# A routed expert kernel: the first token search without its filler products, its grids on ScalarE, and a second expert whose later weight loads wait for its rows

## The chip, the cores and the metric

The kernel runs on one core of a Trainium2 chip. It is one program, launched once. The metric is the device time of one execution in microseconds. Engines are named as in the profile: PE is TensorE, DVE is VectorE, ACT is ScalarE, POOL is GpSimd and SP is SyncE, which here only issues transfers.

## What is computed

An attention stage, then a routing that gives every token one of eight experts, then the experts, then a second feed-forward stage with shared weights, in float32:

```python
x = attention(q, k, v, M_prev, z_prev, beta)      # 4 x 576 tokens, 8 heads of 64
logits = x @ w_gate                               # 2304 tokens, 8 experts
for idx in argsort(-logits.flatten()):            # best pair of token and expert first
    tok, e = divmod(idx, 8)
    if token not assigned and counts[e] < 288:
        assigned[tok] = e; counts[e] += 1
for e in range(8):
    out[mask_e] = maximum(x[mask_e] @ w1[e], 0) @ w2[e]
h = maximum(maximum(out @ m2w1, out @ m2w2), out @ m2w3)
y = h @ m2wo
```

## The kernel before

The program has two parts. `attention` computes the tokens' rows `x` (sent to HBM as `xd`) and their logits `L`. The second part, `routing` and `experts`, runs eight rounds: in each, a search on DVE and PE finds which expert fills up next and which 288 tokens it gets; three indirect transfers on POOL (the gathers, L1223) fetch those tokens' rows; PE transposes them (L1270); then come the two products of the expert (`h1` into `w`, `y` into `acc`) and the second stage (`m2` into `w`, `o` into `acc`). Every product is three matmuls (L1282 to L1284), since each operand is split into a high and a low part: ACT rounds the high part and DVE subtracts it.

**What sets the order.** The parts are written as tasks with a key, costs on their engines and the tasks they depend on (`plan.add`, `plan.op`). `Plan.run` simulates the engines with these costs and writes out one fixed order per engine, and each engine's queue is in order. A changed cost, key or latency therefore changes the order that is written. `GLAT` is the latency that the planner assumes behind a gather, `WLAT` behind a weight load, and `R1KEY` the key at which the second round's search stands.

**The search.** A round has several steps. One step compares all tokens' best logits with a grid of thresholds (`cq`, L1003, in the first round three pieces of 6 token blocks), counts on PE how many lie above each for each expert (L1011, six matmuls per piece), compares the counts with the room left (`fl`, L1015), sums the flags on PE (L1021), takes the maximum (`n1`, L1030) and shifts the logits (`res`, L1032). The next step needs the shifted logits, so the steps are one chain. The first round has six steps of 32 thresholds; its grids `kst` and negated steps `ns` are written by POOL (L964 and L980), apart from the first grid, which DVE writes. A last pass numbers the chosen tokens (L1074, L1082) and gives the row numbers `tidx` (L1088) for the gathers. Before the first step the largest logit `am` goes through PE twice (L941, L955) to reach all partitions.

**The filler.** `NFILL` products of a tile of ones with itself (L1178) are planned wherever PE would be free during the first round's search, and 18 more (`PRE`) stand ahead of it. Nobody reads their result.

**Raw weight pieces.** During attention the second stage's weights, which lie in HBM as 64-bit numbers, are read in 24 pieces into `m2raw` (one buffer) and turned into float32 by one ACT (L818) and three DVE operations (L822, L825, L828). An expert's own weights come in eight pieces of 512 KB (`wraw`, three buffers, L1241) issued by SP. For the first expert only, pieces 3 and later wait for the gathered rows (`FL0`, `tg0`).

Of the kernel before, what the change touches and what calls it, by code (L numbers as in the profile page):

```python
# [17 lines left out]
try:  # L18
# [4 lines left out]
F32 = mybir.dt.float32  # L23
# [22 lines left out]
FL0 = 3  # L46
NFILL, PRE = 398, 18
R1, R1KEY = 9, 15
# [3 lines left out]
GLAT, WLAT = 2500, 6000  # L52
# [4 lines left out]
        "nmt": 2, "PT": 2, "st": 5, "r5": 2, "tmp": 1, "rm": 2, "x": 2, "g": 2, "m2raw": 1, "m2a": 1, "m2b": 1}  # L57
# [3 lines left out]
        "T": (-1.2, 4.7, 5.8), "qj": "POOL", "nslack": 600, "A": (4.1, 6.4, 7.6, 8.7, 8.8), "norm": 15.3, "gate": 6, "m2": (0.0, 5.9, 13.5),  # L61
# [781 lines left out]
def routing_consts(g, tc, consts):  # L843
# [7 lines left out]
    g.iota = iota("iota_row", [128], [[1, 128]], 1)  # L851
    g.w8 = iota("w8", [E], [[-1, E]], E)
# [31 lines left out]
def routing(g, tc, plan, rt, rps, L):  # L884
# [74 lines left out]
    def Q(c, f, r, w):  # L959
        return plan.op(at(), {"POOL": c}, lambda e: f(), r.split(), w.split())  # L960

    def grid(i, s, on=Q, v=nc.gpsimd):
        n, b = PLANS[i]
        on(180 + 1.2 * 2 ** b, lambda: v.tensor_scalar(  # L964
            kst[i][:, s], g.iota[:, :2 ** b], -2.0 ** (b - 1) if s == 0 else -1.0 if s == n - 1 else 0.0, st[i][:, s:s + 1],
            op0=OP.add, op1=OP.mult), f"st{i}", f"kst{i}{s}")

    for i in range(2):
        V(65, lambda i=i: v.tensor_scalar(st[i], g.pw[i], am, None, op0=OP.mult), "am", f"st{i}")
        if i == 0:  # L970
            grid(0, 0, V, v)
# [4 lines left out]
    for i, (n, b) in enumerate(PLANS):  # L976
        for s in range(n):
            if i or s:
                grid(i, s)
            Q(180, lambda i=i, s=s: nc.gpsimd.tensor_scalar(ns[i][:, s], st[i][:, s:s + 1].to_broadcast([128, NB]), -1.0, None,  # L980
                                                            op0=OP.mult), f"st{i}", f"ns{i}{s}")
# [6 lines left out]
    for ph in range(E):  # L988
# [7 lines left out]
        if ph < E - 1:  # L996
# [4 lines left out]
            for s in range(n):  # L1001
                for a in range(0, NB, q):
# [10 lines left out]
                    P(30 * w + (60 if ph else 0), cnt, " ".join(f"cq{x}" for x in range(a + q - w, a + q, q)) + " ohU" +  # L1013
# [59 lines left out]
        for a in range(0, NB, q):  # L1073
# [10 lines left out]
            r.ti = P(46 * w + (60 if ph else 0), idx, " ".join(f"cq{x}" for x in range(a + q - w, a + q, q)) + " mov0 mov1 mov2" +  # L1084
# [26 lines left out]
def experts(g, tc, plan, top, wr, xd, idxd, out):  # L1111
# [60 lines left out]
    def warm(n):  # L1172
        def f(e):
            if not hasattr(fo_, "t"):
                ps.tile([128, 512], F32, name="w", bufs=FBUFS["w"])
                fo_.t = ps.tile([128, 512], F32, name="acc", bufs=4)
            for _ in range(n):
                nc.tensor.matmul(fo_.t[:, :128], g.ones, g.ones, start=True, stop=True)  # L1178
        return f
# [359 lines left out]
```

## Time and profile before

| What | Value |
|---|---|
| median of 3 runs | 874.17 us (873.16 to 878.25) |
| the profiled execution, device time | 874.84 us |
| the profiled execution, span of the core | 872.1 us |
| PE busy | 834.8 us, 96% of the span |
| DVE busy | 553.7 us, 63% |
| ACT busy | 338.9 us, 39% |
| POOL busy | 108.1 us, 12% |
| mean granted PE clock | 0.986 of full speed |

The 2.7 us between the profiled time and its span lie outside the core's instructions. The span has four stretches: attention up to about 266 us, the first search and the gathers of the first expert up to about 309 us, then the experts up to about 866 us, then the last stores. A line of the timeline gives start, duration, engine, line of the kernel, operation, output and inputs, the count of merged instructions, and in brackets how long the engine had idled and for whom. PE's matmuls overlap in it, so a group's duration is the issue of all of them and the drain of the last.

### The profile page before, as it was taken

How to read it: one execution, taken by the hardware profiler on the slowest of the kernel's cores; microseconds unless marked ns; L12 is line 12 of the kernel's file. 1: busy time of each engine (PE TensorE's matmuls, PEld its weight loads, DVE VectorE, ACT ScalarE, POOL GpSimd, SP SyncE). 2: the span in 40 equal slices, each digit the busy share in tenths (PEclk: the TensorE clock that was granted, in tenths of full speed). 3: DMA queues.
4: the chain of work that ended last, by engine and by line, in shares of the span. 5: the costliest groups of instructions: out<-in, count | busy, mean ns of one | idle time of the engine just before them, and what ended most of it. 6: DMA issues, size and time to landing. Idle time of an engine off the chain costs nothing.

```text
span 872.1 us, 18532 instructions
## 1 busy us (share of the span) xinstructions
PE 834.8 (96%) x7234; PEld 770.8 (88%) x7234; DVE 553.7 (63%) x1607; ACT 338.9 (39%) x843; POOL 108.1 (12%) x257
## 2 busy tenths in 40 slices
PE   8899999999997999979999999999999999999996
PEld 6788888888887898869999999999999999999996
DVE  7577777878756796947884783773675552532321
ACT  2566656656555332213313313412412422422311
POOL 2221121123113200202002002002002001000001
PEclk9999999999998999979999999999999999999998
DMA  5445554554323560504403403401421441430000
GB/s 152 142 132 175 167 155 134 187 168 137 122 72 104 140 152 6 170 28 135 111 1 125 121 2 100 126 22 64 145 50 52 145 50 52 145 49 26 25 1 36
DMA packets 39288, 85.59 MB, mean 98 GB/s; under 512 B 11552, under 2 KB 13728, under 8 KB 39200
## 3 DMA queue, kind: packets, MB, share of 16 engines
q1 hardware_dynamic: 35648, 72.87, 29.4%
q0 software_dynamic: 3552, 11.54, 4.6%
q8 instruction: 56, 0.92, 0.4%
q14 instruction: 32, 0.26, 0.1%
HBM read 72.77 MB, written 9.45 MB: 94 GB/s over the span
## 4 chain that ended last, share of the span: by engine, by line
PE 70%; issue 16%; DVE 7%; ACT 4%; POOL 1%; DMA 1%; DVEq 0%; POOLq 0%; ACTq 0%
PE av L622 12%; PE w L1282 9%; PE w L1284 9%; PE w L1283 9%; PE st L582 5%; PE acc L1282 4%; PE acc L1283 4%; PE acc L1284 4%; PE mem L529 3%; PE mem L481 2%; ACT x L552 2%; PE acc L1178 2%; PE rps L1011 2%; DMA xg<-xd,tidx 1%; ACT pt L608 1%
## 5 line engine op out<-in xcount | busy, mean ns | idle before, releaser
L1282 PE MATMUL w<-yh,mh 128*128 128x288 f32 x576 | 174.1, 302 | 0.0
L1284 PE MATMUL w<-yh,ml 128*128 128x288 f32 x576 | 170.0, 295 | 0.0
L1283 PE MATMUL w<-yl,mh 128*128 128x288 f32 x576 | 169.7, 295 | 0.0
L622 PE MATMUL av<-V,pt 128*128 128x112 f32 (+1 forms) x960 | 112.1, 265 | 0.3 <-DVE r L689 0.3
L1282 PEld LDWEIGHTS w<-yh,mh 128*128 128x128 f32 x576 | 109.0, 189 | 2.6
L1283 PEld LDWEIGHTS w<-yl,mh 128*128 128x128 f32 x576 | 108.6, 189 | 2.8
L622 PEld LDWEIGHTS av<-V,pt 128*128 128x128 f32 (+1 forms) x960 | 98.2, 173 | 13.4 <-issue 8.5
L1284 PEld LDWEIGHTS w<-yh,ml 128*128 128x128 f32 x576 | 108.5, 188 | 0.0
L1252 DVE TENSOR_TENSOR wlo<-wraw,whi 128x1024 fp32r<-128x1024 f32 x64 | 78.2, 1222 | 32.3 <-ACT whi L1248 32.3
L1389 DVE TENSOR_TENSOR mt<-w,mt 128x288 f32<-128x288 f32 x96 | 43.6, 455 | 79.2 <-PE w L1284 77.3
L422 DVE CUSTOM_DVE_ANT_0 junk<-st,mask 128x512 bf16<-128x512 f32 (+2 forms) x144 | 66.2, 460 | 30.3 <-PE st L409 20.7
L1283 PE MATMUL acc<-hl,whi 128*128 128x288 f32 x256 | 76.1, 297 | 1.3 <-DVE hl L1197 0.9
L1248 ACT CAST whi<-wraw 128x1024 fp32r<-128x1024 f32 x64 | 67.1, 1049 | 24.5 <-PE acc L1283 16.2
L1284 PE MATMUL w<-xhi,wlo 128*128 128x288 f32 x256 | 75.7, 296 | 0.9 <-DVE wlo L1252 0.9
L1282 PE MATMUL acc<-hh,whi 128*128 128x288 f32 x256 | 76.2, 298 | 0.0
L1282 PE MATMUL w<-xhi,whi 128*128 128x288 f32 x256 | 75.9, 296 | 0.1
L1283 PE MATMUL w<-xlo,whi 128*128 128x288 f32 x256 | 75.5, 295 | 0.0
L1284 PE MATMUL acc<-hh,wlo 128*128 128x288 f32 x256 | 75.3, 294 | 0.0
L1130 ACT CAST gc<-mt 128x32 fp32r<-128x32 f32 (+2 forms) x72 | 17.5, 243 | 141.5 <-DVE mt L1389 141.5
L1223 POOL DMA_INDIRECT xg<-xd,tidx x24 | 25.0, 1042 | 353.4 <-PE w L1284 181.1
L1197 DVE SCALAR_TENSOR_TENSOR hl<-w,hh 128x288 fp32r<-128x288 f32 x64 | 29.1, 456 | 60.2 <-ACT hh L1191 60.2
L608 ACT ACTIVATE pt<-st 128x512 f32<-128x512 f32 x96 | 52.3, 605 | 24.5 <-PE st L582 23.6
(233 smaller groups left out, 1771.4 us busy)
## 6 DMA issues: line engine op xcount, KB each, us to landing
wraw<-in_wr SPq DMA_DIRECT2D x64, 512.0 KB
m2raw<-in_m2w SPq DMA_DIRECT2D x12, 512.0 KB
V<-in_v SPq DMA_DIRECT2D x16, 365.0 KB
KR<-in_kN SPq DMA_DIRECT2D x16, 288.0 KB
QN<-in_qN SPq DMA_DIRECT2D x16, 288.0 KB
VT<-in_vT SPq DMA_DIRECT2D x16, 288.0 KB
xd<-x SPq DMA_DIRECT2D x16, 256.0 KB
m2raw<-in_m2w SPq DMA_DIRECT2D x12, 256.0 KB
```

The costliest lines, as they stand in the source:

```text
L422: V.tensor_tensor_reduce(out=junk[:, :w], in0=o.s[x][:, c:c + w], in1=m, scale=1.0, scalar=-3.0e38, op0=OP.add, op1=OP.max, accum_out=r.nm ...
L529: PE.matmul(MEM[:m, 2 * C * jj:2 * C * jj + 2 * C], r.phi[:, 128 * j:128 * j + m], r.MZ, start=True, stop=True)
L582: PE.matmul(d[:kr, c:c + z - a], neg[q, :kr] if wt is None else wt[q, k], mv[q, a:z], start=x == 0, stop=x == 3)
L608: A.activation(r.PT[:, i, 512 * gi:512 * gi + 512], o.t[i], AF.Exp, scale=0.125)
L622: PE.matmul(AV[:m, i, j * C:j * C + w], r.PT[:, i, o:o + m], r.V[:, c:c + w], start=kb == 0, stop=kb == j)
L1197: V.scalar_tensor_tensor(lo(), src(), 0.0, hi().bitcast(F32), op0=OP.max, op1=OP.subtract)
L1248: A.copy(x.W[fb][0], x.RAW[fb])
L1252: V.tensor_sub(x.W[fb][1], x.RAW[fb], x.W[fb][0].bitcast(F32))
L1282: nc.tensor.matmul(o, wh, rh, start=start, stop=False)
L1283: nc.tensor.matmul(o, wh, rl, start=False, stop=False)
L1284: nc.tensor.matmul(o, wl, rh, start=False, stop=stop)
L1389: V.tensor_max(q.mt, o.pt[:, :T], q.mt)
```

## The change

Six things change. The 18 products ahead of the search and those inside it go: 88 products of ones are left, and each may start only behind the last numbering matmul of the first round. The planner's costs of the first round's matmuls are raised. All 20 operations that write grids and negated steps go to ACT; as ACT's scaling takes no offset, three shifted rows of integers are made once by POOL during attention. `m2raw` gets a second buffer and its conversions other keys. Pieces 3 and later of the second expert wait for that expert's gathers too. `GLAT` is 8500 for all experts but the first, and `R1KEY` 12.

```diff
-NFILL, PRE = 398, 18
-R1, R1KEY = 9, 15
+NFILL = 88
+R1, R1KEY = 9, 12
...
-GLAT, WLAT = 2500, 6000
+GLAT, WLAT = 8500, 6000
...
-        "nmt": 2, "PT": 2, "st": 5, "r5": 2, "tmp": 1, "rm": 2, "x": 2, "g": 2, "m2raw": 1, "m2a": 1, "m2b": 1}
+        "nmt": 2, "PT": 2, "st": 5, "r5": 2, "tmp": 1, "rm": 2, "x": 2, "g": 2, "m2raw": 2, "m2a": 1, "m2b": 1}
...
-"m2": (0.0, 5.9, 13.5),
+"m2": (4, 6.0, 10),
...
+    g.shift = [iota(f"iota{i}", [n], [[1, n]], 1 - a, dt=BF) for i, (n, a) in enumerate([(2 ** b, 2 ** (b - 1)) for _, b in PLANS] + [(128, 1)])]
...
     def Q(c, f, r, w):
-        return plan.op(at(), {"POOL": c}, lambda e: f(), r.split(), w.split())
-
-    def grid(i, s, on=Q, v=nc.gpsimd):
+        return plan.op(at(), {"ACT": c}, lambda e: f(), r.split(), w.split())
+
+    def grid(i, s):
         n, b = PLANS[i]
-        on(180 + 1.2 * 2 ** b, lambda: v.tensor_scalar(
-            kst[i][:, s], g.iota[:, :2 ** b], -2.0 ** (b - 1) if s == 0 else -1.0 if s == n - 1 else 0.0, st[i][:, s:s + 1],
-            op0=OP.add, op1=OP.mult), f"st{i}", f"kst{i}{s}")
+        x = g.iota if 0 < s < n - 1 else g.shift[i if s == 0 else 2]
+        Q(170 + 0.89 * 2 ** b, lambda: nc.scalar.mul(kst[i][:, s], x[:, :2 ** b], st[i][:, s:s + 1]), f"st{i}", f"kst{i}{s}")
...
         if i == 0:
-            grid(0, 0, V, v)
+            grid(0, 0)
...
-            Q(180, lambda i=i, s=s: nc.gpsimd.tensor_scalar(ns[i][:, s], st[i][:, s:s + 1].to_broadcast([128, NB]), -1.0, None,
-                                                            op0=OP.mult), f"st{i}", f"ns{i}{s}")
+            Q(190, lambda i=i, s=s: nc.scalar.mul(ns[i][:, s], st[i][:, s:s + 1].to_broadcast([128, NB]), -1.0), f"st{i}", f"ns{i}{s}")
...
-                    P(30 * w + (60 if ph else 0), cnt, " ".join(f"cq{x}" for x in range(a + q - w, a + q, q)) + " ohU" +
+                    P((30 if ph else 50) * w + (60 if ph else 0), cnt, " ".join(f"cq{x}" for x in range(a + q - w, a + q, q)) + " ohU" +
...
-            r.ti = P(46 * w + (60 if ph else 0), idx, " ".join(f"cq{x}" for x in range(a + q - w, a + q, q)) + " mov0 mov1 mov2" +
+            r.ti = P((46 if ph else 95) * w + (60 if ph else 0), idx, " ".join(f"cq{x}" for x in range(a + q - w, a + q, q)) + " mov0 mov1 mov2" +
...
-    tf = add(-2000, {"PE": 1}, warm(PRE), new=[bfl])
     for k in range(NFILL):
-        add(1e5 + k, {"PE": 56}, warm(1), [tf], use=[bfl])
+        add(1e5 + k, {"PE": 75}, warm, [g.rounds[0].ti], new=[] if k else [bfl], use=[bfl] if k else [])
...
-                          [r.tt], new=[bg] if c == 0 else [], use=[bg] if c else [], lat=GLAT))
-        if p == 0:
-            tg0 = tg
+                          [r.tt], new=[bg] if c == 0 else [], use=[bg] if c else [], lat=GLAT if p else 2500))
...
-                if p == 0 and fb == FL0:
+                if p < 2 and fb == FL0:
...
-            t0 = add(kw + FK["load"] + .1, {"SP": 2000}, fl, [x.tvl] + (tg0 if p == 0 and fb >= FL0 else []), new=[br], lat=WLAT)
+            t0 = add(kw + FK["load"] + .1, {"SP": 2000}, fl, [x.tvl] + (tg if p < 2 and fb >= FL0 else []), new=[br], lat=WLAT)
```

The order shows what the planner made of this at three places. The first is DVE at the end of attention, from the last logits to the first operation of the search (`am`); `tmp` and `x` are the last head's rows. Before, and then now:

```order
L707 TENSOR_TENSOR L<-L,lg_3877 64x8
L723 TENSOR_TENSOR tmp<-av,r_3861 128x10x64
L727 TENSOR_TENSOR x<-x,tmp 128x2x5x64
L822 TENSOR_SCALAR m2b<-m2raw 128x512
L825 SCALAR_TENSOR_TENSOR m2b<-m2a,m2b 128x512
L828 SCALAR_TENSOR_TENSOR w_80<-m2raw,m2b 128x512
L939 TENSOR_REDUCE am<-L 128x1
```

```order
L707 TENSOR_TENSOR L<-L,lg_3889 64x8
L723 TENSOR_TENSOR tmp<-av,r_3873 128x10x64
L727 TENSOR_TENSOR x<-x,tmp 128x2x5x64
L940 TENSOR_REDUCE am<-L 128x1
```

The last conversion of a raw piece stands no longer between them; the last of the 24 conversions now stands some 60 DVE instructions ahead of `am`, and the first some 35 earlier than before.

The second is PE from the spreading of `am` to the first count (27 products of ones stand where the line of dots is), and now the same and, behind the dots, the end of the first round up to the transposes of the first expert's rows (`xg`):

```order
L955 MATMUL rps<-one_3094,am_3917 128x1
L1178 LDWEIGHTS ones
L1178 MATMUL acc<-ones 128x128
...
L1011 LDWEIGHTS cq
L1011 MATMUL rps<-ohU,cq 32x8
```

```order
L942 MATMUL rps<-ident,am 1x128
L956 MATMUL rps<-one_3132,am_3923 128x1
L1010 LDWEIGHTS cq
L1010 MATMUL rps<-ohU,cq 32x8
...
L1081 MATMUL rps<-mov,cq 96x6
L1095 LDWEIGHTS ones
L1095 MATMUL rps<-rab,ones 128x8
L1174 LDWEIGHTS ones
L1174 MATMUL acc<-ones 128x128
...
L1010 MATMUL rps<-ohU,cq 128x8
L1261 MATMUL w<-ident,xg 128x96 x12
```

No product of ones is left in the search; all 88 stand in one piece behind it, and behind them the 18 counts of the second round's first step and then the transposes, as before (where the piece of ones there had 107). On ACT the first plan's twelve grid operations stand behind two of the twelve casts of the second stage's weights, the other eight behind the last of these casts; the accumulating transfers of POOL (L1157), which were behind POOL's grids, keep their places against the gathers.

The third is PE between the second round's numbering matmuls and the transposes of the second expert's rows, before and now:

```order
L1082 MATMUL rps<-mov,cq 96x6
L1282 MATMUL w<-yh,mh_3970 128x288
...
L1284 MATMUL w<-yh,ml 128x288
L1270 MATMUL w<-ident,xg 128x96 x3
```

```order
L1081 MATMUL rps<-mov,cq 96x6
L1273 MATMUL w<-yh,mh_3977 128x288
...
L1275 MATMUL w<-yh,ml 128x288
L1261 MATMUL w<-ident,xg 128x96 x3
```

Before, 66 matmuls of 288 columns, 6 of 512 and 18 counts stand at the dots; now 90 of 288, 18 of 512 and 36 counts. From the transposes of the third expert on, PE's order is the same in both.

## Rows read from the trace of the kernel before

**Rows 1.** Windows: stretch, its length, busy us per engine, granted PE clock, DMA share, GB/s.

```profile
276.00:277.00 1.00, 1.00 (x12) 0.95 (x9) 0.00 (x0) 1.00 (x2) 1.00 (x5) 0.50 0.00 0
...
372.00:373.00 1.00, 0.00 (x0) 0.00 (x0) 0.00 (x0) 0.00 (x0) 0.00 (x0) 0.81 0.00 0
...
382.00:383.00 1.00, 1.00 (x4) 0.76 (x4) 0.98 (x2) 0.00 (x0) 0.00 (x0) 0.57 0.00 0
...
390.00:500.00 110.00, 109.93 (x921) 105.41 (x920) 79.44 (x219) 37.74 (x82) 9.84 (x13) 1.00 0.34 97
```

**Rows 2.** Timeline, from the end of attention to the search's first count.

```profile
269.13 0.42 DVE L822 TENSOR_SCALAR m2b<-m2raw 128x512 int32<-128x512 int32 x1
...
270.99 0.29 DVE L939 TENSOR_REDUCE am<-L 128x1 f32<-128x144 f32 x1
...
272.26 0.13 DVE L953 TENSOR_SCALAR am<-am 1x1 int32<-1x1 int32 x1
...
273.65 0.58 PE L955 MATMUL rps<-one,am 1*128 1x1 f32 x2
...
274.16 3.04 PE L1178 MATMUL acc<-ones 128*128 128x128 bf16 x27
...
275.00 0.91 DVE L1003 TENSOR_TENSOR cq<-m,kst 128x192 bf16<-128x192 f32 x3
...
277.92 0.31 PE L1011 MATMUL rps<-ohU,cq 128*32 128x8 bf16 x6
```

**Rows 3.** Timeline, later steps of the first round's search.

```profile
279.92 1.36 DVE L1003 TENSOR_TENSOR cq<-res,kst 128x192 bf16<-128x192 f32 x3
...
283.05 0.90 DVE L1003 TENSOR_TENSOR cq<-res,kst 128x192 bf16<-128x192 f32 x3
...
284.28 0.31 PE L1011 MATMUL rps<-ohU,cq 128*32 128x8 bf16 x6
...
284.63 0.15 DVE L1015 TENSOR_TENSOR fl<-rps,R 32x8 bf16<-32x8 f32 x1 [0.68 <-PE rps L1011]
...
285.07 0.17 PE L1021 MATMUL rps<-fl,ones 32*128 32x8 bf16 x1
...
291.61 0.90 DVE L1003 TENSOR_TENSOR cq<-res,kst 128x192 bf16<-128x192 f32 x3
...
293.93 0.17 DVE L1030 TENSOR_REDUCE n<-rps 128x1 f32<-128x8 f32 x1 [0.58 <-PE rps L1027]
```

**Rows 4.** Timeline, from the end of the first round to the first expert's transposes.

```profile
300.18 6.13 PE L1178 MATMUL acc<-ones 128*128 128x128 bf16 x107
...
300.55 0.16 DVE L1088 SCALAR_TENSOR_TENSOR tidx<-rps,ixs 96x3 int32<-96x3 f32 x1
...
306.91 1.08 PE L1270 MATMUL w<-ident,xg 96*128 96x96 f32 x9
```

**Rows 5.** Timeline, the second expert's row numbers, gathers and transposes.

```profile
357.15 0.93 PE L1082 MATMUL rps<-mov,cq 128*96 128x6 bf16 x18
...
366.55 1.27 POOL L1223 DMA_INDIRECT xg<-xd,tidx  x1 [0.31 <-issue]
...
375.12 0.42 PE L1270 MATMUL w<-ident,xg 96*128 96x96 f32 x1 [5.73 <-DMA xg<-xd,tidx]
...
376.47 0.42 PE L1270 MATMUL w<-ident,xg 96*128 96x96 f32 x1 [0.93 <-DMA xg<-xd,tidx]
```

**Rows 6.** Tile view of `xhi`, 370 to 400 us: durations min/median/max, first and last start.

```profile
L1282 PE MATMUL w<-xhi,whi x14: 292/295/378, 389.7 to 399.0; 128*128 128x288 f32 x14
```

**Rows 7.** Source view of the gathers, all 24 of them.

```profile
DMA to landing us min/median/max: 3.0/3.1/11.2
```

**Rows 8.** Waits, 20 to 266 us: us in total, times, longest.

```profile
PE st L582 <- ACT pt L608: 8.9, 14, 1.1
```

**Rows 9.** Groups on ACT: count | busy us, mean ns | idle before.

```profile
L1130 ACT CAST gc<-mt 128x32 fp32r<-128x32 f32 (+2 forms) x72 | 17.5, 243 | 141.5 <-DVE mt L1389 141.5
...
L1147 ACT CAST mh<-w 128x1024 fp32r<-128x1024 f32 x12 | 11.6, 1038 | 0.0
```

More of the change, by code (lines that the diff above doesn't have):

```diff
@@ L60 @@
 PRIO = {"load": -24, "prep": -17, "low": -9.5, "S": -18.6, "ds": 2.6, "N": -8.8, "G": -6, "phi": -4.5, "mem": (0.7, 5.0), "memx": "ACT",
-        "T": (-1.2, 4.7, 5.8), "qj": "POOL", "nslack": 600, "A": (4.1, 6.4, 7.6, 8.7, 8.8), "norm": 15.3, "gate": 6, "m2": (0.0, 5.9, 13.5),
+        "T": (-1.2, 4.7, 5.8), "qj": "POOL", "nslack": 600, "A": (4.1, 6.4, 7.6, 8.7, 8.8), "norm": 15.3, "gate": 6, "m2": (4, 6.0, 10),
         "tmg": (1, 6, 9, 12)}
@@ L1170, in experts, with warm @@
     bfl, fo_ = Buf(R["acc"]), K()
[L1172 to L1179, printed above, removed]
-    tf = add(-2000, {"PE": 1}, warm(PRE), new=[bfl])
+    def warm(e):
+        if not hasattr(fo_, "t"):
+            fo_.t = ps.tile([128, 512], F32, name="acc", bufs=4)
+        nc.tensor.matmul(fo_.t[:, :128], g.ones, g.ones, start=True, stop=True)
     for k in range(NFILL):
-        add(1e5 + k, {"PE": 56}, warm(1), [tf], use=[bfl])
+        add(1e5 + k, {"PE": 75}, warm, [g.rounds[0].ti], new=[] if k else [bfl], use=[bfl] if k else [])
     g.scat = []
@@ L1206, in experts @@
     E_ = [K() for _ in range(E)]
-    tg0 = []
     prev = None
```

## The prediction

> **What bounds the kernel now.** I read the windows first. From 390 to 500 us PE is busy 109.93 of 110 us [rows 1], and PE's order from the third expert on is untouched, so nothing there can be won or lost. Two stretches are left in which PE's work is not the bound. One is the first search, from the first operation on the logits at 270.99 us [rows 2] to the transposes of the first expert's rows at 306.91 [rows 4]: 35.9 us in which PE does little that anybody reads. The other is the second expert's start, where PE reaches the transposes and waits 5.73 and 0.93 us for two gathers [rows 5]. PE is the bound again right behind both, so what is saved in either shortens the kernel by as much. In the timeline of these stretches the reader is to look, in each step of the chain, for time between the end of one operation and the start of the next on the other engine: that is where a product of ones, a DVE conversion or a late transfer sits.
>
> **The conversions leave the tail.** `am` starts at 270.99 behind the conversion that begins at 269.13 [rows 2]; with none there it starts at 269.13: 1.86 us. The work itself moves into attention, where the 24 conversions are spread over as many DVE instructions as before, only some 35 to 60 earlier. I cost that at nothing. What covers it there is PE's own work; PE waited for exponentials on ACT 8.9 us in 14 waits [rows 8], and I allow 1.5 us either way.
>
> **The first products of ones go.** DVE has the reduced `am` ready at 272.39 (272.26 + 0.13), PE runs its matmul at 273.65 [rows 2]. With an empty queue about 0.1 us of hand-over is left: 1.15 us saved. POOL's and DVE's writing of grids becomes ACT's: an ACT operation on 32 to 96 columns takes 0.243 us on average [rows 9], DVE's first grid took about the same, and the hand-overs add at most 0.2 us; I take zero.
>
> **The steps.** A step of the search lasts (291.61 - 283.05) / 3 = 2.85 us undisturbed [rows 3]: 0.90 for the comparisons, 0.64 from their end (283.95) to the end of the third count (284.59), 0.19 to the end of the flags (284.78), 0.29 to the sum of the flags (285.07), 0.83 for the maximum, the shift and the hand-overs to the next comparison. Without ones in the queue the third count starts about 0.1 us behind its comparison and the sum 0.1 us behind the flags. At the clock of before the step would be 0.90 + 0.1 + 0.31 + 0.19 + 0.1 + 0.83 = 2.43 us.
>
> But the clock will not be that of before. In the window at 276 us it was granted at 0.50, the lower of PE's two levels (1.2 GHz), after PE had stood idle at the end of attention, and 27 products of ones then took 3.04 us, 0.112 each; at the upper level 107 took 6.13, 0.057 each [rows 1, 2, 4]. It rose only after PE had worked without a break. In the changed search PE has 18 small counts per step and waits in between, so I take the lower level for all of it. What a count costs there, no row shows. A group of six takes 0.31 us at the upper level [rows 3], of which some 0.04 us each is issue and the rest drain. Lower bound: nothing more. Upper bound: its issue doubles as that of the ones did, 0.47 per group, more than the 0.30 of a comparison; PE then paces the step, with 0.30 + 0.1 + 3 x 0.47 + 0.17 of drain to the end of the third count and 0.05 more in the sum: 3.14 us. I take 2.65, nearer to the lower end, because the issue of a count with 8 columns does not follow its columns: 0.04 against 0.057 for 128.
>
> The first step lasted 275.00 to 279.92, 4.92 us, with the count behind 27 ones (277.92), and the second 3.13, with comparisons of 1.36 instead of 0.90 us beside POOL's grids [rows 2, 3]. Gains: 4.92 - 2.65 = 2.27; 3.13 - 2.65 = 0.48; three steps of 0.20, 0.61 together; the last, from 291.61 to the maximum at 293.93, 0.22. The numbering behind it has 18 matmuls at the lower clock, of which the last six are not covered: 0.25 us lost. Row numbers: 1.86 + 1.15 + 2.27 + 0.48 + 0.61 + 0.22 - 0.25 = 6.3 us earlier, 300.55 becomes 294.2.
>
> **The 88 products behind the search.** They start where the 107 did, 300.18 - 6.3 = 293.9, and stand ahead of the counts and the transposes. After the second expert's wait the clock was still below full 6 us after PE had taken up work at 376.47 (0.57 in the window at 382 us) [rows 1, 5]. By that, 54 ones at 0.112 take 6.0 us and 34 at 0.057 another 1.9, ending at 301.8; with 0.6 for the counts the transposes start at 302.5. The rows themselves would be there at 306.91 - 6.3 = 300.6 [rows 4]: now the ones are late, not the gathers. The first product comes 306.91 - 302.5 = **4.4 us** earlier. Bounds: 9.9 us if all 88 run at 0.112, 5.0 if none does.
>
> ACT's other work is hidden: twenty grid operations are 4.9 us of ACT, which held only casts that are needed from the second stage on. They delay the third accumulating transfer, which stands ahead of the gathers in POOL's queue and behind twenty grid operations, ten casts and three negations on ACT: from the steps' values at about 271.5 that is 20 x 0.243 + 13 x 1.04 us later [rows 9], 289.9, against the new `tidx` at 294.2. Beyond these 4.3 us each us of delay is a us of the kernel.
>
> **The second expert.** Its numbering matmuls stood at 357.15, the last gather landed with the transpose at 376.47, 19.3 us later [rows 5]; the shortest landing of a gather is 3.0 us, the median 3.1, the longest 11.2 [rows 7]. Between the two PE now has 90 matmuls of 288 columns at 0.133 (the spacing in the trace), 18 of 512 at 0.229, 36 counts and the numbering itself: 18.2 us of its own work, where it had 12.0 (357.15 to 369.15). And SP's loads of pieces 3 and later, which were under way when the gather of 366.55 was issued, now wait for it. So the wait goes: 5.73 + 0.93, and with it the lower clock up to about 382.5, in which 6 us of work took the place of 3: together **9.7 us**. SP has only this expert's other pieces and its row numbers for the stores behind the waiting load. The first product is at 389.7 [rows 6], 13.2 us behind the last transposed rows; before the fourth piece is needed, 72 matmuls of the first product and at least 48 of the second run, some 16 us. Late next would be that piece, and its cover is long.
>
> **A rule against the change.** The Trainium skill (TensorE: Matmul & The Clock Gate, What's actually happening) says that the throttled state is the default and activity lifts it; by that, taking the ones out leaves the search at half rate. The rows at 276 us agree on the two rates. If everything PE does in the search doubled by it, the sum would be that of the second rival below.
>
> **The sum.** 4.4 + 9.7 = 14.1 us. The profiled execution took 874.84 us, 0.67 above the median of 874.17; 860.7 for the one, 860.1 for the other.
>
> **The rivals.**
> - *The gathers of the second expert are slow for another reason.* For it: from 372 us on no transfer moves (DMA share 0.00) and the gathers are still out [rows 1]; against it: the 3.1 us of the others [rows 7]. The Trainium skill (DMA: Bandwidth & Descriptors, Queues, rings and completion order) says that an engine takes turns between its queues, so that loads should slow a gather, not stop it. A gather as slow as before still meets 18.2 us of work instead of 12.0, a wait of 1.1 us: 861.2. Chance 0.12.
> - *The clock takes the search's gain back.* Steps of 3.14 us: the gains are 1.86 + 1.15 + 1.78 + 0 - 0.86 - 0.25 - 0.5 = 3.2, the ones start at 297.0, all at 0.112 for 9.9 us, counts at double 1.2: transposes at 308.1, 1.2 us later than before. 874.17 + 1.2 - 9.7 = 865.7. Chance 0.11.
> - *The clock holds.* Steps of 2.43, no lost end: the rows come 7.7 us earlier and the ones end in time. 874.17 - 7.7 - 9.7 = 856.8. For it only that the idle stretch before the search is shorter; chance 0.06.
> - *The second expert's wait does not go*, because neither loads nor place decided it: 874.17 - 4.4 = 869.8. Against it are the 6.2 us of added cover; chance 0.07.
> - *Slower: attention pays for the conversions.* One ACT and three DVE operations come in front of exponentials and maxima that PE waits for. A wait is 0.64 us (8.9 / 14) [rows 8]; it needs 22 new ones, nearly one for each of the 24 conversions, to use up 14.1 us, and gives 874 and more. Against it: the same work already ran there at the same density. Chance 0.04.
>
> **The numbers.** The forecast has 0.60; its own bounds (attention, the ones, the count) are 857 to 864. From 856 to 867 lie the forecast, the first three rivals and no more of the others: 0.85 or so. This measurement tells a change from none at about 1%, 8.7 us. Faster by more: the forecast, the first and third rival, 0.78; within: the second and fourth, 0.18; slower 0.04.
>
> **What would show it.** `am` follows directly on the last `x`; the first comparisons follow `st` within 0.6 us; the third count starts 0.1 us behind its comparison; the steps repeat at 2.4 to 2.8 us at a granted clock of 0.5; the ones run 0.112 apart for some 6 us and end just ahead of the transposes; at the second expert no wait for `xg`, and a clock of 1.00 through it. I am wrong if the steps grow to 3 us, if PE stands ahead of the counts for `ohU` or of the transposes for a late gather, or if attention ends more than 2 us away from 266.

## The result and the profile after

The changed kernel takes 864.46 us (median; 863.53 to 865.19), the kernel before, run beside it, 874.97 us (873.16 to 878.25, one run more than in the 874.17 above): a ratio of 0.9875, 95% interval 0.9843 to 0.9907. It is faster, by 1.25%; 860.1 us was forecast, so 4.4 us of the gain are missing. The profiled execution took 863.53 us, with a span of 861.8 against 872.1.

The windows of the changed kernel, which answer to [rows 1] (columns as there), with four stretches more:

```profile
276.00:277.00 1.00, 0.00 (x0) 0.00 (x0) 0.75 (x4) 1.00 (x2) 0.02 (x1) 0.50 0.56 106
294.00:295.00 1.00, 1.00 (x16) 1.00 (x15) 1.00 (x3) 0.00 (x0) 1.00 (x1) 0.77 1.15 270
301.00:302.00 1.00, 0.00 (x0) 0.00 (x0) 1.00 (x3) 0.51 (x1) 0.00 (x0) 0.65 0.68 131
307.00:308.00 1.00, 1.00 (x6) 1.00 (x5) 1.00 (x2) 0.00 (x0) 0.00 (x0) 0.50 0.20 70
336.00:337.00 1.00, 1.00 (x6) 0.85 (x6) 0.51 (x3) 0.00 (x0) 0.00 (x0) 0.50 0.00 0
372.00:373.00 1.00, 1.00 (x26) 0.82 (x21) 0.78 (x3) 0.95 (x4) 0.00 (x0) 1.00 0.00 0
382.00:383.00 1.00, 1.00 (x10) 0.97 (x10) 0.62 (x6) 0.00 (x0) 0.00 (x0) 1.00 0.42 91
390.00:500.00 110.00, 109.93 (x923) 105.49 (x922) 76.29 (x190) 36.51 (x83) 7.72 (x10) 1.00 0.33 93
```

The hole at 372 us is closed and the clock behind it full. New are two stretches at the lower clock, at 307 and at 336 us, where the kernel before ran at 1.00:

```profile
307.00:308.00 1.00, 0.99 (x11) 0.71 (x9) 0.62 (x2) 0.42 (x2) 0.00 (x0) 1.00 1.03 201
336.00:337.00 1.00, 1.00 (x9) 1.00 (x8) 1.00 (x2) 0.52 (x2) 0.00 (x0) 1.00 0.03 8
```

The timeline of the changed kernel through the start of the search, against [rows 2, 3]:

```profile
269.16 0.29 DVE L940 TENSOR_REDUCE am<-L 128x1 f32<-128x144 f32 x1
...
270.53 0.57 PE L956 MATMUL rps<-one,am 1*128 1x1 f32 x2 [0.66 <-DVE am L954]
...
271.95 0.90 DVE L1002 TENSOR_TENSOR cq<-m,kst 128x192 bf16<-128x192 f32 x3 [0.26 <-ACT kst L966]
...
272.36 0.86 PE L1010 MATMUL rps<-ohU,cq 128*32 128x8 bf16 x18 [1.26 <-DVE cq L1002]
...
274.32 0.89 DVE L1002 TENSOR_TENSOR cq<-res,kst 128x192 bf16<-128x192 f32 x3
```

No product of ones stands ahead of anything; a step is 274.32 - 271.95 = 2.37 us, the later ones 2.33, at a granted clock of 0.50. From `am` to the row numbers it is now 22.89 us, where it was 29.56. Then, from the row numbers to the first product, against [rows 4] (rows that are not part of the chain are left out):

```profile
291.68 6.39 PE L1174 MATMUL acc<-ones 128*128 128x128 bf16 x88
292.05 0.16 DVE L1087 SCALAR_TENSOR_TENSOR tidx<-rps,ixs 96x3 int32<-96x3 f32 x1
...
298.57 1.06 ACT L1153 ACTIVATE ml<-mh 128x1024 fp32r<-128x1024 f32 x1 [10.41 <-DMA ml<-w]
299.54 1.97 ACT L1239 CAST whi<-wraw 128x1024 fp32r<-128x1024 f32 x2
300.60 1.23 DVE L1243 TENSOR_TENSOR wlo<-wraw,whi 128x1024 fp32r<-128x1024 f32 x1 [4.05 <-ACT whi L1239]
301.74 0.30 DVE L949 TENSOR_TENSOR ohU<-w,mx 128x144 bf16<-128x144 f32 x1
302.09 0.62 PE L1010 MATMUL rps<-ohU,cq 128*128 128x8 bf16 x18 [4.02 <-DVE ohU L949]
302.57 2.57 PE L1261 MATMUL w<-ident,xg 96*128 96x96 f32 x12
...
305.24 0.59 PE L1273 MATMUL w<-xhi,whi 128*128 128x288 f32 x1
```

These nine lines are a chain of waits, to be read from the bottom. PE stood 4.02 us ahead of the second round's counts for the one-hot rows `ohU`; `ohU` stood on VectorE behind a low part `wlo`; that waited 4.05 us for ScalarE's cast `whi`; and the cast stood on ScalarE behind the fourth negation, which had waited 10.41 us for the third accumulating transfer. The rows had all landed by 299.9, and in a run below that takes the negation away the first cast starts at 290.72: the weights had been there too. PE stood idle from 298.07; its clock fell at 301.3, and the first products ran at 0.50.

The second expert, against [rows 5]:

```profile
353.00 0.93 PE L1081 MATMUL rps<-mov,cq 128*96 128x6 bf16 x18
...
361.58 0.92 POOL L1216 DMA_INDIRECT xg<-xd,tidx  x1 [0.30 <-issue]
...
371.60 0.41 PE L1261 MATMUL w<-ident,xg 96*128 96x96 f32 x3
```

There is no wait for `xg` any more. The source view of all the changed kernel's gathers, against [rows 7] (the longest, 6.5 us, is one of the first expert's), its waits in attention, against [rows 8], and the new groups on ScalarE, whose price I had taken from [rows 9] as 243 ns:

```profile
DMA to landing us min/median/max: 3.0/3.1/6.5
```

```profile
PE st L582 <- ACT pt L608: 8.7, 13, 1.0
```

```profile
L980 ACT ACTIVATE ns<-st 128x18 f32<-128x18 f32 x10 | 2.0, 201 | 0.0
L966 ACT ACTIVATE kst<-iota_row,st 128x32 bf16<-128x32 f32 (+1 forms) x6 | 2.0, 332 | 0.0
```

In attention PE waits about as much as before, and the twenty small operations cost ScalarE 5.4 us (the four other grids are 1.4), near the 4.9 that I had taken.

### The profile page after: what moved, and what is told of

Read it like the earlier page. It is cut to its first block, busy times and chain, and to the rows that moved or that the text cites. A ratio compares the mean times of both kernels' runs of the same rounds, so it can differ in the third digit from the quotient of the medians.

```text
span 861.8 us, 17857 instructions
## 1 busy us (share of the span) xinstructions
PE 814.8 (95%) x6906; PEld 754.0 (87%) x6906; DVE 553.1 (64%) x1606; ACT 342.5 (40%) x863; POOL 102.6 (12%) x241
## 4 chain that ended last, share of the span: by engine, by line
PE 72%; issue 16%; ACT 5%; DVE 4%; DMA 2%; POOL 1%; POOLq 0%; DVEq 0%; ACTq 0%
PE av L622 12%; PE w L1273 10%; PE w L1275 9%; PE w L1274 9%; PE st L582 5%; PE acc L1273 5%; PE acc L1274 5%; PE acc L1275 5%; PE mem L529 3%; PE mem L481 2%; DMA ml<-w 2%; ACT x L552 2%; PE rps L1010 1%; PE st L409 1%; PE av L738 1%
```

## The experiments

All medians are in us; each ratio is to runs of the kernel before on the same chip (their medians were 875.4, 876.9, 877.3 and 875.1 in the four groups of runs). The other columns are from the profiled execution. The place of `am` moves between executions (268.5 to 272.3 us in the twelve profiles with the changed kernel's code ahead of it), so I cut each profile in two at the start of `tidx`: "search" is from `am` to `tidx`, "rest" from `tidx` to the end of the span. The last three columns count from `tidx` to the first, 144th and 192nd of the experts' products.

| kernel | median | ratio, 95% | search | rest | 1st | 144th | 192nd |
|---|---|---|---|---|---|---|---|
| before | 874.97 | | 29.56 | 571.55 | 8.5 | 29.6 | 36.9 |
| changed | 864.46 | 0.9875 (0.9843-0.9907) | 22.89 | 569.75 | 13.2 | 35.5 | 45.9 |
| exp2only | 866.87 | 0.9894 (0.9868-0.9920) | 28.57 | 561.94 | 8.5 | 29.6 | 36.8 |
| searchonly | 871.30 | 0.9929 (0.9903-0.9956) | 22.91 | 577.79 | 12.9 | 35.7 | 46.5 |
| noexp2wait | 866.53 | 0.9885 (0.9848-0.9922) | 22.76 | 570.01 | 13.0 | 35.7 | 44.9 |
| kd3 | 863.97 | 0.9866 (0.9839-0.9893) | 22.92 | 569.55 | 13.1 | 37.1 | 44.6 |
| acclat | 869.66 | 0.9918 (0.9889-0.9948) | 22.76 | 576.81 | 10.6 | 32.2 | 46.6 |
| ones148 | 864.16 | 0.9855 (0.9827-0.9884) | 22.77 | 570.58 | 12.9 | 35.6 | 45.8 |
| acc3lat | 862.62 | 0.9828 (0.9795-0.9861) | 22.91 | 569.07 | 10.6 | 37.7 | 45.6 |
| kd2 | 860.32 | 0.9807 (0.9774-0.9840) | 22.91 | 566.55 | 10.3 | 34.2 | 41.6 |
| idxonly | 863.70 | 0.9847 (0.9821-0.9872) | 22.78 | 569.98 | 13.1 | 35.7 | 45.8 |
| acc3idx | 859.34 | 0.9801 (0.9774-0.9827) | 23.02 | 562.74 | 9.7 | 30.7 | 39.2 |
| kd2idx | 859.31 | 0.9792 (0.9764-0.9820) | 23.03 | 564.17 | 10.2 | 32.0 | 39.4 |
| gridpool | 858.51 | 0.9810 (0.9787-0.9834) | 22.97 | 563.96 | 9.8 | 32.5 | 40.4 |

The bookkeeping of the changed kernel is in the first three lines: `am` 1.83 us and the search 6.67 us earlier, the second expert 571.55 - 561.94 = 9.61 us, together 18.1; the span fell by 10.3. So **7.8 us are given back** between the row numbers and the end (569.75 against 561.94). The four kernels below that differ from the changed one without helping or harming it (noexp2wait, kd3, ones148, idxonly) have a rest of 569.55 to 570.58, so on the changed kernel's side the number is no accident of one profile. The 192nd product stands at 337.93 us, in the kernel before at 337.40: by then all that the first part of the change had gained is gone, and the 10.3 us are the second expert's 9.61 and little else. The experiments ask where it went.

### The parts of the change

**exp2only.** The kernel before with the second expert's part alone.

```diff
-GLAT, WLAT = 2500, 6000
+GLAT, WLAT = 8500, 6000
...
-                          [r.tt], new=[bg] if c == 0 else [], use=[bg] if c else [], lat=GLAT))
+                          [r.tt], new=[bg] if c == 0 else [], use=[bg] if c else [], lat=GLAT if p else 2500))
...
-                if p == 0 and fb == FL0:
+                if p < 2 and fb == FL0:
...
-            t0 = add(kw + FK["load"] + .1, {"SP": 2000}, fl, [x.tvl] + (tg0 if p == 0 and fb >= FL0 else []), new=[br], lat=WLAT)
+            t0 = add(kw + FK["load"] + .1, {"SP": 2000}, fl, [x.tvl] + (tg if p < 2 and fb >= FL0 else []), new=[br], lat=WLAT)
```

> The kernel before with the second expert's part of the change alone: its later weight loads wait for its gathers, and the planner takes 8.5 us for those gathers. Theory: the stall of 5.7 and 0.9 us and the 3 us at the lower clock behind it go, nothing else: 874.97 less 9.7, 865 to 866.5 us. Rival (the freed time is lost again later, to weights that come late): 869 to 874, with PE waiting for low parts of weights behind 375.

Measured: 866.87, a little above the theory's range, and in the profile 9.61 us less behind `tidx`. The transposes find their rows, and the clock stays:

```profile
372.00:373.00 1.00, 1.00 (x23) 0.89 (x22) 0.17 (x1) 0.00 (x0) 0.00 (x0) 1.00 0.00 0
382.00:383.00 1.00, 1.00 (x10) 1.00 (x9) 1.00 (x2) 0.00 (x0) 0.00 (x0) 1.00 0.00 0
```

The term of 9.7 us holds.

**searchonly.** The changed kernel with those edits taken back.

> The changed kernel without the second expert's part: its loads do not wait for its gathers, and the planner takes 2.5 us for those as before. What is left of the change is the search (no products of ones in it, grids on ScalarE) and the buffers of the conversions. If the parts add, it is the kernel before less what the changed kernel gained over the second expert's part alone: 875.4 less 2.4, 872 to 874 us, although its row numbers come 8 us earlier. Rival (the search part is worth its forecast 4.4 us and the second expert's part hides some of it): 870 to 871.5.

Measured: 871.30, a little under the theory's range and inside the rival's. In the profile the search is 6.65 us shorter and the rest 6.24 us *longer* than before: in this profile the search part pays for itself and keeps almost nothing. Its ratio, 0.9929, is a gain of 6.2 us (3.8 to 8.5), more than the 2.9 us by which this profile's span is shorter, so how much it keeps is open. The stall of 5.6 us at the second expert is back.

**noexp2wait.** The changed kernel in which only the loads no longer wait for the gathers; the planner's 8.5 us stay.

```diff
-                if p < 2 and fb == FL0:
+                if p == 0 and fb == FL0:
...
-            t0 = add(kw + FK["load"] + .1, {"SP": 2000}, fl, [x.tvl] + (tg if p < 2 and fb >= FL0 else []), new=[br], lat=WLAT)
+            t0 = add(kw + FK["load"] + .1, {"SP": 2000}, fl, [x.tvl] + (tg if p == 0 and fb >= FL0 else []), new=[br], lat=WLAT)
```

> The changed kernel in which the second expert's loads do not wait for its gathers, while the planner still takes 8.5 us for these. It tells whether the wait or the planner's number takes the stall away. If the gathers were slow because of the loads beside them (11.2 us in the kernel before), they are slow again here; the planner then has other products ahead of the transposes, which hide about 8 of the 11 us: 864.5 to 868 us. If the wait is what counts and the planner's number nothing: 871 to 874 us.

Measured: 866.53, the rest 570.01 against 569.75, no difference. The second expert's gathers are slow again, and nobody minds (source view of the gathers between 340 and 385 us, first in the changed kernel, then in noexp2wait, and noexp2wait's timeline):

```profile
DMA to landing us min/median/max: 3.1/3.4/3.8
DMA to landing us min/median/max: 4.5/5.6/10.5
```

```profile
371.70 0.55 PE L1261 MATMUL w<-ident,xg 96*128 96x96 f32 x4 [0.17 <-DMA xg<-xd,tidx]
```

So the loads do slow the second expert's gathers (4.5 to 10.5 us with them, 3.1 to 3.8 without), but what takes the stall away is the order: 19.1 us of other work between the numbering (352.60) and the transposes. The wait itself bought nothing that shows.

**gridpool** (on acc3idx below, where a gain in the search reaches the end). Grids and step sizes on GpSimd again, the first grid on VectorE.

```diff
-        return plan.op(at(), {"ACT": c}, lambda e: f(), r.split(), w.split())
+        return plan.op(at(), {"POOL": c}, lambda e: f(), r.split(), w.split())
...
-            grid(0, 0)
+            grid(0, 0, V, v)
...
-            Q(190, lambda i=i, s=s: nc.scalar.mul(ns[i][:, s], st[i][:, s:s + 1].to_broadcast([128, NB]), -1.0), f"st{i}", f"ns{i}{s}")
+            Q(180, lambda i=i, s=s: nc.gpsimd.tensor_scalar(ns[i][:, s], st[i][:, s:s + 1].to_broadcast([128, NB]), -1.0, None,
+                                                            op0=OP.mult), f"st{i}", f"ns{i}{s}")
```

> The kernel acc3idx, in which what the search gains reaches the end, with the search's grids and step sizes on GpSimd again (the first grid on VectorE), as in the kernel before; the products of ones stay out. It parts the search's gain into its two halves. Theory (nearly all of it comes from the products of ones that no longer stand ahead of the counts on PE; the grids on ScalarE bring only what VectorE lost beside GpSimd in the first steps, 1.36 in place of 0.90 us for the comparisons and 0.58 in place of 0.24 us for the result, and 0.2 us at the start): the time from the first maximum to the row numbers is 23.1 us or so in place of 23.0 less or more 0.2, plus 0.8 to 1.2 us; 860 to 861 us. Rival (GpSimd holds VectorE or the chain more now that each step is shorter, since its 18 grid instructions then reach into more steps): 2 to 4 us later, 861.5 to 863.5.

Measured: 858.51 and a search of 22.97 us against 23.02. The time alone decides little: the chip was another, and by the ratios (0.9810 against 0.9801) this kernel is 0.8 us slower, which the theory had and which is inside the intervals. The search decides. It has not grown, where the theory wanted about 1 us more and the rival 2 to 4: the grids' move to ScalarE brings nothing, and the search's 6.6 us are there without it. What else left the search's chain are the products of ones; a run with them alone put back was not made. VectorE lost some time beside GpSimd in one step (comparisons of 1.11 us in place of 0.90), and gained about as much at the start, where it has the first grid at once:

```profile
272.38 0.24 DVE L965 TENSOR_SCALAR kst<-iota_row,st 128x32 bf16<-128x32 f32 x1
272.66 0.91 DVE L1004 TENSOR_TENSOR cq<-m,kst 128x192 bf16<-128x192 f32 x3
...
277.44 1.11 DVE L1004 TENSOR_TENSOR cq<-res,kst 128x192 bf16<-128x192 f32 x3
```

### Where the 7.8 us went

**kd3.** The fourth low part on VectorE, no fourth negation.

```diff
-KD = 4
+KD = 3
```

> The changed kernel with the fourth low part computed by VectorE, like the eight behind it, in place of ScalarE's fourth negation and the transfer that adds to it. Theory: the changed kernel has its row numbers 8.5 us earlier, but ScalarE, in order, stands 10.4 us at the fourth negation until the third accumulating transfer has landed (298.6), so the first weight casts, the second round's one-hot rows and with them PE come no earlier than 302.1. Without that negation the first cast stands at about 295, the transposes start when the gathers are in (298.5 to 299.5), and PE's clock has no idle 4 us to fall in: 4 us for the start and up to 3 for the clock, 858 to 860.5 us. Rival (the gathers or the weight pieces hold PE to 302 anyway, ScalarE's wait is covered): 863.5 to 865. Rival (VectorE, with one more low part, becomes what the first products wait for): 862 to 866, with waits for low parts of weights.

Measured: 863.97, no change (rest 569.55), inside both rivals. ScalarE was free (first cast at 290.72), the transposes began at 299.13, and then the same transfer caught PE through VectorE:

```profile
298.65 1.23 DVE L1160 TENSOR_TENSOR ml<-w,mh 128x1024 fp32r<-128x1024 f32 x1 [4.47 <-DMA ml<-w]
299.79 0.30 DVE L947 TENSOR_TENSOR e<-e,w 128x144 f32<-128x144 f32 x1
...
304.48 0.74 PE L1261 MATMUL w<-ident,xg 96*128 96x96 f32 x3 [3.60 <-DVE xlo L1193]
```

Each low part is written over the weights that the one before it reads (`slot`), so the fourth waits for the third transfer whichever engine computes it. The wait only changed engines.

**acclat.** The planner's time for every accumulating transfer at 10.5 us.

```diff
-            low = add(FK["m2"] + k + .2, {"POOL": 1100}, facc, [low], lat=4500)
+            low = add(FK["m2"] + k + .2, {"POOL": 1100}, facc, [low], lat=10500)
```

> The changed kernel with the planner's time for an accumulating transfer at 10.5 us in place of 4.5; so ScalarE has two weight casts ahead of the third negation, and POOL the gathers ahead of the third accumulating transfer. Theory (ScalarE's wait at the fourth negation ends the time of the first casts): the wait is gone from ahead of the casts, transposes at about 298 to 299, 858 to 861 us; the gathers, without that transfer beside them, land in 4 us or less. Rival (the wait is covered): 863.5 to 865. If the two negations now stand ahead of work that is waited for later, the gain is smaller, and ScalarE shows waits for a transfer behind 305.

Measured: 869.66, worse, against both expectations (the intervals of the ratios overlap a little, but the rest is 7.1 us longer). The first product did come 2.6 us sooner, but the third negation, too, went behind casts, the low parts came late, and VectorE was full when PE needed it (windows, and the timeline behind them):

```profile
330.00:336.00 6.00, 3.09 (x35) 2.63 (x34) 6.00 (x8) 0.41 (x1) 0.00 (x0) 1.00 0.00 0
336.00:342.00 6.00, 4.72 (x25) 4.16 (x24) 6.00 (x11) 1.60 (x4) 0.00 (x0) 0.72 0.01 3
```

```profile
344.24 0.61 PE L1274 MATMUL w<-yl,mh 128*128 128x288 f32 x1 [3.52 <-DVE yl L1193]
```

**ones148.** The last 60 products of ones made twice, to fill PE's idle 4 us.

```diff
-        nc.tensor.matmul(fo_.t[:, :128], g.ones, g.ones, start=True, stop=True)
+        for _ in range(2 if k >= 28 else 1):
+            nc.tensor.matmul(fo_.t[:, :128], g.ones, g.ones, start=True, stop=True)
```

> The changed kernel with its last 60 products of ones made twice each, so that at 0.057 us each they fill 3.4 of the 4.0 us that PE stands idle before the transposes; nothing else moves. It separates the lost clock from the lost start. Theory: the wait stays (transposes at 302.5), but the granted clock stays at 1.00 through 302 to 308, where it was 0.50: transposes about 1.2 us shorter, and the first 23 products of 288 columns at 0.13 in place of 0.24, 2.5 us: 861 to 862.5 us. Rival (the first products wait for weights and low parts anyway, so that a faster clock only makes longer waits): 863.8 to 865.

Measured: 864.16, no gain (rest 570.58). The ones ran to 302.5, but PE then waited 0.8 us for `ohU` and 0.6 for `xlo`, and the clock fell all the same:

```profile
301.00:302.00 1.00, 1.00 (x22) 1.00 (x20) 0.20 (x1) 1.00 (x2) 0.87 (x1) 1.00 0.00 0
304.00:305.00 1.00, 0.69 (x9) 0.50 (x7) 0.67 (x3) 0.72 (x3) 0.00 (x0) 1.00 1.15 188
306.00:307.00 1.00, 1.00 (x5) 1.00 (x6) 0.73 (x4) 1.00 (x2) 0.00 (x0) 0.50 1.03 418
```

It does not settle what the clock alone is worth, since it did not hold the clock.

**acc3lat.** 11.5 us for the third transfer alone: the fourth negation goes behind the first casts, and ahead of the first products nothing else moves.

```diff
-            low = add(FK["m2"] + k + .2, {"POOL": 1100}, facc, [low], lat=4500)
+            low = add(FK["m2"] + k + .2, {"POOL": 1100}, facc, [low], lat=4500 if k != 2 else 11500)
```

> The changed kernel with the planner's time for the third accumulating transfer alone at 11.5 us in place of 4.5, about what it took (10.0): ScalarE's fourth negation then stands behind the first two weight casts and the casts of the rows, and nothing else moves ahead of the first products. Theory A (ScalarE's wait in order at the fourth negation is what makes the second half of the search's gain vanish): first weight cast at about 291 in place of 299.5, VectorE without its idle 4 us at 296.5 to 300.6, transposes at about 299, first product at 302 in place of 305.2, and the 3 us stay to the end: 860.5 to 862. Theory B (VectorE's low parts and the second round's comparisons bound the first expert up to 340, and the clock falls whenever PE has to wait): the first product comes earlier, but the products of 320 to 340 do not: 863 to 865, with PE waiting for low parts of weights and comparisons, and a stretch at the lower clock.

Measured: 862.62, between the two theories, and in the profile a rest of 569.07, only 0.7 us less. ScalarE's wait is gone, the first product comes 10.6 us behind `tidx` in place of 13.2 and the first 24 take 3.14 us in place of 4.44, at full clock. Yet the 144th product is *later*. Neither theory named the cause; it is on SP's queue:

```profile
306.98 0.80 SPq L1346 DMA_DIRECT2D idxd<-tidx  x1
317.84 0.41 SPq L1350 DMA_DIRECT2D idx<-idxd  x1
318.50 3.21 SPq L1232 DMA_DIRECT2D wraw<-in_wr  x1
...
325.96 0.61 PE L1273 MATMUL w<-xhi,whi 128*128 128x288 f32 x1 [4.33 <-ACT whi L1239]
```

SP stores the row numbers (1.1 KB) at 306.98, and its next instruction reads them back. It stands 10 us until they have landed, and the last weight pieces stand behind it. PE waits 4.33 us, then runs at 0.50 again.

**kd2.** The third and fourth low part on VectorE; no transfer is left beside gathers and weights.

```diff
-KD = 4
+KD = 2
```

> The changed kernel with two low parts, the third and the fourth, moved from ScalarE and transfers to VectorE (10 of 12 there): no accumulating transfer is left beside the gathers and the weight pieces, and VectorE has no transfer to wait for. VectorE then gets 2 times 1.14 us more, into 4 us in which it stood idle. Theory A (waiting for the transfer): gathers land in 3 to 5 us, transposes at about 297 to 299, first product at 301 to 302, 860 to 862 us. Theory B (VectorE bounds): the low parts stand ahead of those that the first products need, 862 to 866, with PE waiting for VectorE ahead of 320.

Measured: 860.32, as Theory A had it; the rest is 566.55, 3.2 us less than in the changed kernel, although VectorE has two low parts of 1.2 us more to compute. The first product is 2.9 us sooner. The first 24 still ran at the lower clock (5.7 us), behind a wait of 1.9 us for the gathers.

**acc3idx, kd2idx, idxonly.** One SP instruction, the first expert's read-back, behind its last two weight loads: on acc3lat, on kd2, and on the changed kernel.

```diff
-        x.tidx = add(k0 + FK["idx"] + .1, {"SP": 500}, fj, [t], lat=2300)
+        x.tidx = add(k0 + FK["idx"] + .1, {"SP": 500}, fj, [t] + ([] if p else x.tl[7:]), lat=2300)
```

> The kernel acc3lat with one SP instruction moved: the first expert's read-back of its row numbers stands behind the last two weight loads instead of ahead of them. In acc3lat SP stood 10.0 us at this read-back for the store of the same numbers (issued at 306.98, read back at 317.84), the last weight pieces were issued only at 318.5, PE waited 4.3 us for the seventh piece's cast and then ran at the lower clock; the 96th to the 144th product took 13.1 us, where the kernel before took 7.9. Theory (the search's gain runs into the next fixed wait, this round trip): the wait goes, with it the stretch at the lower clock, 5 us at the 144th product; to the end 4 to 6 us of it: 856.5 to 859. Rival (VectorE bounds the first expert up to 340 anyway): the time comes back as waits for low parts and comparisons ahead of 345: 860.5 to 862.6.

> The kernel kd2 with the same instruction moved. There SP stood 9.3 us at the read-back, but PE waited only 0.7 us for the pieces behind it, since VectorE's low parts came first. Theory (what bounds here is VectorE and the clock of the first products, not the weights): 0.5 to 1 us, 859 to 860.5 us. Rival (the round trip costs here too): 856 to 858.

> The changed kernel with this instruction moved and nothing else. Its SP stood 3.4 us at the read-back, and PE waited 1.25 us for the low part of the eighth piece, ahead of which VectorE is busy without a break from 310.8 to 328.6. Theory (in the changed kernel ScalarE's wait at the fourth negation and VectorE bound, and the round trip is not yet reached): 0 to 1 us, 863.5 to 865. Rival (the round trip already bounds): 860 to 862.

Measured: acc3idx 859.34, kd2idx 859.31, idxonly 863.70. The last two are as their theories had it in time, though kd2idx's rest is 2.4 us shorter than kd2's, more than its theory's 1. acc3idx is by its median 0.3 us above its theory's range, but its profile, in which `tidx` happened to come 3.3 us later than in the changed kernel's, has a rest of 562.74, 7.0 us less. The SP rows of acc3idx:

```profile
309.64 0.68 SPq L1346 DMA_DIRECT2D idxd<-tidx  x1
313.99 1.47 SPq L1232 DMA_DIRECT2D wraw<-in_wr  x2
318.65 0.39 SPq L1350 DMA_DIRECT2D idx<-idxd  x1
```

The last pieces are issued 18.6 us behind `tidx`, where it was 26.7 in acc3lat, and from `tidx` to 347 us PE waits nowhere longer than 0.6 us. With the changed kernel, acc3lat, idxonly and acc3idx stand as a square: rest 569.75, 569.07, 569.98, 562.74. **In these profiles either wait taken away alone gives 0.7 or nothing; both together give 7.0 of the 7.8 us.** gridpool, which has both edits too, has 563.96, 5.8 us less. By medians, too, acc3idx (0.9774 to 0.9827) lies clear of the changed kernel (0.9843 to 0.9907): that the two waits cost most of what was lost is shown. That either alone brings next to nothing rests on one profile each, and the times do not bear it out. The ratios of the four are 0.9875, 0.9828, 0.9847 and 0.9801, gains of 4.1 and 2.5 us alone and 6.5 together, each uncertain by some 4 us; two gains that simply add fit them as well. And acc3lat's fastest execution has a span of 858.2 us; with the earliest `am` of any profile (268.5) it leaves a rest of at most 566.8, so its rest varies by more than 2 us. acc3idx, kd2idx and gridpool beat both kernels, and their intervals do not tell them apart.

## Why the prediction was right, and where it was not

The sign and the range held; the mechanism held for the larger part, the second expert (9.61 us measured, 9.7 forecast), and failed for the smaller, the search: of its 4.4 us some 0.7 are left at the end (10.3 less 9.61).

**The conversions.** `am` starts at 269.16, forecast 269.13. That place moves by up to 3.8 us between executions, but it moves together with the last `x`: from the start of that operation to `am` it is 2.6 us in both profiles with the conversion between them (before, exp2only) and 0.74 in all twelve without. So the 1.86 us are shown. Whether attention up to the last `x` pays for them is not: it starts at 268.4 and 271.6 in the two, and from 267.8 to 271.6 in the twelve.

**The first products of ones.** With `am` in its place the first comparisons were due at 275.00 - 1.86 - 1.15 = 271.99; they start at 271.95. Right.

**The steps were mis-sized, to the good.** 2.65 us were forecast, 2.33 measured, below my lower bound of 2.43. The clock was the lower one, as I took it (0.50), but the counts of eight columns did not follow it. A group of six spans 0.32 us, at the upper clock 0.31 [rows 3]:

```profile
274.74 0.32 PE L1010 MATMUL rps<-ohU,cq 128*32 128x8 bf16 x6 [1.08 <-DVE cq L1002]
```

Inside it the counts start 0.027 us apart, in the kernel before 0.025; the 0.04 that I took for their issue was too much at either clock. From the comparisons' end (275.21) to the end of the flags (275.78) it is 0.57 us, where my lower bound had 0.60; from there to their sum 0.06, where I took 0.1; and 0.82 from the sum to the next comparison, where I had 0.83. So the unknown price lay at its lower end, and the hand-overs through PE were shorter still. The Trainium skill (TensorE: Matmul & The Clock Gate, What's actually happening) calls the throttled state the default; the clock granted here, 0.50, agrees. A doubling of all that PE does, as in the second rival, was a bad price for these small products. The row numbers came 8.5 us earlier instead of 6.3, and gridpool shows that the grids had no share in it.

**The ones behind the search.** I gave the clock 6 us to rise; it rose in the window at 294 us, some 3 us after the ones and 5 after the numbering ahead of them had begun, and they ended at 298.07, not 301.8. The transposes then stood at 302.57 where I had said 302.5: the right number by luck, since the ones had long been done and a wait that I had not seen stood in their place.

**The step that failed first: "ACT's other work is hidden".** I asked who stands behind the third transfer on POOL's queue (the gathers) and found 4.3 us of cover; it was issued at 288.46, before `tidx`, so that much was true. I did not ask who waits for its *landing*. It landed after 10.0 us, beside three weight pieces and the gathers, where the other three took 4.6 to 5.3 (tile view of `ml`, 276 to 306 us, of the changed kernel):

```profile
DMA to landing us min/median/max: 4.6/5.2/10.0
```

And ScalarE's next instruction waited for it, with the weight casts behind. The Trainium skill (PSUM — Partial Sum Buffer, Engine vs sequencer instructions) says that ScalarE's queue is strictly first in, first out; the rows at 298.57 and 299.54 agree: the cast stands behind the negation and its 10.41 us. In the kernel before this transfer was issued at 290.50 and had landed at 295.02, ahead of the first weight load (295.80). The faster search pulled the loads 8.5 us forward and the transfer only 2.0, so that they met. The grids on ScalarE had little to do with it: without them, in gridpool, the transfer is issued 4.2 us ahead of `tidx` in place of 3.6. I had named this sign myself, PE ahead of the counts for `ohU`.

**The step that failed second: "PE is the bound again right behind both".** It is so behind the second expert (9.61 us measured, 9.7 forecast), not behind the first. There VectorE, the clock and SP's queue allow PE to go little faster from `tidx` on: in the changed kernel the 192nd product comes 45.9 us behind `tidx`, in the kernel before 36.9. What had been hidden behind PE's slow search now shows. Between 321 and 347 us it is read in these rows of the changed kernel:

```profile
326.27 0.40 PE L1275 MATMUL w<-xhi,wlo 128*128 128x288 f32 x1 [1.25 <-DVE wlo L1243]
...
333.22 0.31 PE L1010 MATMUL rps<-ohU,cq 128*128 128x8 bf16 x6 [0.56 <-DVE cq L1002]
334.09 0.31 PE L1010 MATMUL rps<-ohU,cq 128*128 128x8 bf16 x6 [0.56 <-DVE cq L1002]
```

VectorE was busy without a break from 310.8 to 328.6, the work it had not done in its idle 4 us among it; PE waited three times, and the clock fell behind that to 0.50, as the window at 336 shows.

**The second expert.** The price was right, the reason half. I put the wait's going down to the loads that no longer run beside the gathers, and to the longer cover. The loads are indeed what makes these gathers slow, against the first rival; but noexp2wait shows that the cover alone takes the stall away, as that rival had it (slow gathers, hidden but for 1.1 us; 0.17 us measured).

**The rivals.** "The clock takes the search's gain back" gave 865.7, near the result, but by steps of 3.14 us that did not come. That the clock took part of the gain back, at another place, is seen in the first 24 products (4.44 in place of 3.14 us). How much of the 7.8 us is clock and how much wait stays open.

## What to carry to other kernels

For every instruction that is moved or delayed, ask not only what stands behind it in its own queue but who waits for its completion, and what stands behind *that* in the waiter's queue. When a stage is made faster, look for the next two waits, not one: where two end at nearly the same time, one may show little until the other is gone too. And cut a profile at the end of the stage that was changed: what the stage gained and what the rest lost are then two numbers instead of one small difference.

## What was not expected of the hardware

- An accumulating transfer of 512 KB, which otherwise landed after 4.6 to 5.3 us in the changed kernel, took 10.0 us when issued 1.1 us behind the first of three weight loads of 512 KB each, with the gathers behind them (9.9 to 10.9 us in kd3, searchonly, acc3lat and acc3idx, where it stands the same). Which of its neighbours slowed it was not parted.
- A store of 1.1 KB of row numbers let its read-back go 9.4 us later in the kernel before (313.06 to 322.46), 9.9 in the changed one (309.09 to 319.00) and 10.9 in acc3lat (306.98 to 317.84); the wait that ended last was each time the store's landing. In acc3lat no transfer moved from 311 to 317 us, while SP stood there.
- Matmuls of 8 columns start 0.027 us apart at the lower clock and 0.025 at the upper one, while those of 128 columns doubled (0.107 and 0.056 between starts).
